# A fused attention and two MoE layers on one core: new step order, sums' guards and weight casts on GpSimd, 29 matmuls halved

## The chip, the cores and the metric

The kernel runs on one NeuronCore of one Trainium2 chip. The metric is the device time of one execution in microseconds. TensorE multiplies (its weight loads have a row of their own, PEld); VectorE is DVE, ScalarE is ACT, GpSimd is POOL and SyncE, which issues the DMAs, is SP in the profile.

## What is computed

Two batches of 12 heads of causal attention (448 tokens, 64 numbers a head), then two layers over the 896 tokens: one with a squared relu, one with the maximum of three products.

```python
scores = q @ k.T / 8;  scores[mask] = -1e9
attn = exp(scores - max(scores));  attn /= sum(attn) + 1e-9
x = (attn @ v)                       # 896 x 768 after joining heads
g = maximum(x @ w_in, 0) ** 2        # 896 x 2048
y = g @ w_out                        # 896 x 768
h = maximum(maximum(y @ w1, y @ w2), y @ w3)
out = h @ w_o                        # 896 x 768
```

q, k and v are float32; the weights arrive as float64 and are put together as float32 on the chip.

## The kernel before

**Attention** works on 12 pairs of heads. A pair's steps are scores (s, TensorE), masked row maxima (m, a custom VectorE instruction that also moves the scores from PSUM into `pr`), exponentials with their sums (e, ScalarE, sums into `st`), the guard 1e-9 on the sums and their reciprocals (r, both on VectorE), the norms (n on GpSimd, n' on VectorE: multiply a row block by its reciprocal), transposes (g, TensorE), their move out of PSUM (h on ScalarE, h' on VectorE) and the product with v (w, TensorE). Row blocks 0 to 6 have 128, 128, 256, 256, 384, 384 and 448 columns; the reciprocals come in three groups a pair (NORM). The output of a pair leaves PSUM by xf or xh (rounded high part) and xl (what the rounding left); sums of such blocks (d) get their own high and low parts (1h to 4h, 1l to 4l).

**Three multiplications** (names f, o and h for w_in, w_out and w1 to w3) use a seven-product scheme for two by two blocks. Every operand is split into a rounded high part and a residual, and a product is three passes, so a step M1 to M7 is nine matmuls of 448 columns. A weight block is loaded into `wr`, then C (`Weight.cast`, ScalarE) spreads the 16 bits on top into the single buffer `up`, and J (`Weight.join`, VectorE) joins it with the rest and issues the next weight load on SP. T1 to T4 (VectorE) form sums of blocks. A quarter of a block gets its high part by H (`Quarter.hi`, ScalarE) and its residual by L (`Quarter.lo`, VectorE) in a ring of five buffers `wq`. XH and XL (also YH, YL, WH, WL, ZH, ZL) do the same to the other operands, S, Y and Z form their sums, and V steps bring results out of PSUM. In the second multiplication M1 of blocks 0 to 3 and M3 of blocks 4 to 7 stay in full precision (`run_full`, line 807). The fourth multiplication, with w_o, is written out behind the order.

**The order** of all steps is the table ORDER. Its entries are issued one by one under a manual schedule, so each engine runs its own steps in the order of the table and waits only for its operands and buffers. In a name such as `H.f3M7` the part behind the point is the block and product, in `e4.5` block 4 of pair 5. Loads of q, k and v are tied to the steps s0 and w0.

Of the kernel before, what the change touches and what calls it, by code (L numbers as in the profile page):

```python
# [28 lines left out]
e6.0 m6.1 m0.1 s4.1 r0.0 m1.1 wload n6'.0 e6.1 m4.1 n4.0 e3.0 r1.0 e0.1 n5.0 e1.1 s2.1 n1.0 n2.0  # L29
g3.0 h3.0 s6.2 m2.1 g0.0 n3'.0 n0'.0 e4.1 m5.1 h0.0 m3.1 r2.1 m6.2 e5.1 g2.0 g1.0 h1'.0 n0.1 s4.2  # L30
s0.2 r0.1 m4.2 m1.2 m0.2 h2.0 w0.0 n4.1 e2.1 w1.0 e6.2 m5.2 n5.1 w2.0 e1.2 n1'.1 n6'.1 w3.0 e4.2
e3.1 s2.2 r1.1 s0.3 m2.2 m3.2 g2.1 e5.2 g0.1 e0.2 e2.2 h2.1 xf.0 e3.2 r0.2 r2.2 n0'.2 g3.1 n1'.2
n5'.2 m0.3 s4.3 m1.3 e0.3 e1.3 m4.3 r1.2 h0.1 m5.3 xh.0 n2.1 s2.3 n3.1 n6.2 n4.2 g1.1 n2'.2 h3.1
m3.3 s6.3 h1.1 n3.2 g3.2 s6.4 m2.3 e3.3 h3'.2 m6.3 g2.2 g1.2 g0.2 s2.4 xl.0 r2.3 e5.3 m6.4 n0'.3
e4.3 s0.4 e6.3 e2.3 m2.4 e6.4 m3.4 r1.3 r0.3 e3.4 n2.3 h1'.2 w0.1 m0.4 w1.1 h2.2 m1.4 w2.1 n3.3
e1.4 n5.3 w3.1 n4.3 s4.4 h0'.2 n1'.3 e2.4 s2.5 m4.4 n6'.3 C.i0 r1.4 g1.3 h1.3 g0.3 g3.3 d3.1 e0.4
n2'.4 m5.4 3h.1 s6.5 m3.5 m2.5 e5.4 m6.5 g2.3 e3.5 s4.5 e4.4 r2.4 s0.5 h0'.3 m1.5 w0.2 w1.2 r0.4
m4.5 n0.4 w2.2 n3.4 e6.5 n1.4 h3.3 e1.5 e2.5 n4.4 n6.4 w3.2 h2'.3 m5.5 m0.5 g1.4 e4.5 s6.6 e5.5
# [18 lines left out]
n1'.11 L.f0M6 h0.10 w0.10 C.i5 w1.10 J.i5 T2.f1 n0.11 2h.7 T3.f0 w2.10 w3.10 3h.9 h1.11 g3.11
g2.11 xh.10 xl.10 h0.11 M2b.f1 M2c.f0 M1c.f1 1l.7 h3.11 T3.f1 T1.f2 d4.7 h2.11 xf.10 w0.11 H.f1M6
2l.7 w1.11 H.f1M3 w2.11 L.f1M6 w3.11 M2c.f1 4h.7 C.i7 L.f1M3 d2.11 2h'.11 V0.f1M1 2l.11 H.f0M7
4l.7 more d1.11 xh.11 L.f0M7 H.f0M5 J.i7 M6.f0 1h'.11 3l.9 M6.f1 V0.f0M6 1l.11 M7.f0 L.f0M5 H.f1M7  # L60
T4.f0 C.i6 H.f1M5 L.f1M7 L.f1M5 H.f0M4 V0.f1M6 J.i6 C.i11 T4.f1 M5.f0 M5.f1 H.f3M1 d4.11 L.f0M4
4h.11 M7.f1 V0.f1M2 V0.f0M7 V1.f1M2 J.i11 xl.11 H.f1M4 V0.f1M7 T1.f3 V2.f1M2 L.f1M4 M4.f0 L.f3M1
# [80 lines left out]
def tile_attention_moe_moe(  # L143
# [23 lines left out]
    nc = tc.nc  # L167
# [227 lines left out]
    class Pair:  # L395
# [126 lines left out]
        def steps(self):  # L522
# [11 lines left out]
            for n, c in enumerate(NORM):  # L534
                e[f"r{n}"] = lambda c=c: self.recip(*c)
# [658 lines left out]
```

## Time and profile before

| what | us |
|---|---|
| three runs | 458.04, 457.92, 455.61; median 457.92 |
| the profiled execution | 456.35 |
| its span, first to last instruction | 454.6 |
| TensorE busy | 447.0 (98%) |
| VectorE busy | 396.3 (87%) |
| ScalarE busy | 324.7 (71%) |
| GpSimd busy | 35.3 (8%) |

Records of matmuls overlap, since a matmul's record holds its way through the array; TensorE's rate is read from the start of one to the start of the next, or from a long stretch divided by its count. The granted clock was full (0.999 in the mean).

### The profile page before, as it was taken

The page shows a single profiled execution, that of the slowest core. Times are in us where ns is not written, and L with a number is a line of the kernel's source. Part 1 is how long each engine was busy: PE and PEld are TensorE (multiplying, and loading weights), DVE is VectorE, ACT ScalarE, POOL GpSimd, SP SyncE. Part 2 cuts the span into 40 slices and gives each one's busy share as a digit, 9 for nine tenths or more (in the row PEclk, how much of TensorE's full clock was granted, in tenths as well). Part 3 has the DMA queues.
Part 4 walks back from the last instruction along what each step waited for, and adds up shares of the span by engine and source line. Part 5 has one row for each costly group of instructions (what it writes and reads, how often), then busy time and mean ns, then how long its engine had stood idle before and what let it go on. Part 6 is the DMA issues. An engine that isn't in the chain of part 4 may idle for free.

```text
span 454.6 us, 6911 instructions
## 1 busy us (share of the span) xinstructions
PE 447.0 (98%) x2338; PEld 384.5 (85%) x2338; DVE 396.3 (87%) x900; ACT 324.7 (71%) x712; POOL 35.3 (8%) x72
## 2 busy tenths in 40 slices
PE   8999999999999999999999999999999999999996
PEld 5676656789999999779999999689999999899996
DVE  5999999999776797999999999999787777788963
ACT  5999999868699899887576777575666455652551
POOL 3424551400000000000000000000000000000000
PEclk9999999999999999999999999999999999999999
DMA  7535274436566666452222534364253023000014
GB/s 219 182 110 185 87 252 122 143 131 183 165 160 189 176 171 193 154 141 69 71 69 69 178 101 145 133 209 138 69 164 116 1 74 136 0 2 0 35 54 156
DMA packets 39395, 56.28 MB, mean 124 GB/s; under 512 B 1728, under 2 KB 31552, under 8 KB 39360
## 3 DMA queue, kind: packets, MB, share of 16 engines
q1 hardware_dynamic: 39072, 55.61, 39.5%
q8 instruction: 18, 0.29, 0.3%
q10 hardware_dynamic: 288, 0.23, 0.1%
q14 instruction: 17, 0.14, 0.1%
HBM read 53.08 MB, written 2.75 MB: 123 GB/s over the span
## 4 chain that ended last, share of the span: by engine, by line
PE 82%; DVE 16%; issue 2%; DVEq 0%
PE ps L575 46%; PE ps L800 19%; PE ps L981 5%; PE ps L807 4%; DVE pr L432 4%; PE ps L421 4%; PE ps L460 2%; PE ps L491 2%; DVE z L202 1%; DVE pr L452 1%; DVE piece L195 1%; DVE wd L202 1%; DVE s L202 1%; DVE wd L255 1%; DVE ph L483 1%
## 5 line engine op out<-in xcount | busy, mean ns | idle before, releaser
L575 PE MATMUL ps<-s,wq 128*128 128x448 f32 x612 | 129.8, 367 | 0.0
L575 PEld LDWEIGHTS ps<-s,wq 128*128 128x128 f32 x612 | 114.7, 188 | 10.6 <-issue 0.4
L575 PE MATMUL ps<-a,wq 128*128 128x448 f32 x459 | 101.2, 369 | 0.3 <-DVE a L195 0.2
L575 PEld LDWEIGHTS ps<-a,wq 128*128 128x128 f32 x459 | 85.3, 188 | 9.2 <-DVE wq L195 0.8
L800 PE MATMUL ps<-x,wq 128*128 128x448 f32 x432 | 88.7, 367 | 0.0
L800 PEld LDWEIGHTS ps<-x,wq 128*128 128x128 f32 x432 | 81.1, 188 | 7.1 <-issue 0.6
L250 ACT CAST up<-wr 128x768 f16<-128x768 bf16 x56 | 60.1, 1074 | 9.3 <-DVE wd L255 2.9
L192 ACT CAST wq<-wd 128x384 fp32r<-128x384 f32 x91 | 45.9, 511 | 25.8 <-PE ps L575 13.1
L255 DVE SCALAR_TENSOR_TENSOR wd<-wr,up 128x768 int32<-128x768 int32 x56 | 54.0, 964 | 9.3 <-ACT up L250 9.3
L195 DVE TENSOR_TENSOR wq<-wd,wq 128x384 fp32r<-128x384 f32 x91 | 49.4, 554 | 7.9 <-ACT wq L192 7.6
L192 ACT CAST wq<-wt 128x384 fp32r<-128x384 f32 x68 | 34.4, 512 | 22.3 <-PE ps L575 20.9
L440 ACT ACTIVATE pr<-pr,st 128x128 f32<-128x128 f32 (+3 forms) x84 | 44.0, 527 | 6.4 <-DVE st L432 6.0
L195 DVE TENSOR_TENSOR wq<-wt,wq 128x384 fp32r<-128x384 f32 x68 | 36.8, 556 | 12.1 <-ACT wq L192 12.0
L432 DVE CUSTOM_DVE_ANT_0 pr<-ps,mask 128x128 f32<-128x128 f32 (+3 forms) x84 | 34.9, 445 | 4.1 <-PE ps L421 3.7
L421 PE MATMUL ps<-k,q 64*128 64x384 f32 (+3 forms) x168 | 36.4, 450 | 1.4 <-DVE st L432 1.2
L452 POOL TENSOR_SCALAR pr<-pr,st 128x384 f32<-128x384 f32 (+3 forms) x59 | 32.8, 570 | 50.2 <-DVE st L448 24.7
L585 ACT COPY s<-ps 128x448 f32<-128x448 f32 x38 | 20.0, 529 | 13.1 <-PE ps L575 11.9
L421 PEld LDWEIGHTS ps<-k,q 64*128 64x128 f32 (+1 forms) x168 | 19.0, 195 | 11.0 <-DVE st L432 5.9
L460 PEld LDWEIGHTS ps<-ident,pr 128*128 128x128 f32 x192 | 21.4, 140 | 7.1 <-issue 3.7
L460 PE MATMUL ps<-ident,pr 128*128 128x128 f32 x192 | 26.3, 277 | 0.0
L195 DVE TENSOR_TENSOR x<-g,x 128x448 fp32r<-128x448 f32 x40 | 24.3, 620 | 0.0
L491 PE MATMUL ps<-ph,v 128*64 128x448 f32 (+3 forms) x192 | 23.4, 386 | 0.5 <-DVE a L195 0.3
(115 smaller groups left out, 568.0 us busy)
## 6 DMA issues: line engine op xcount, KB each, us to landing
wr<-in_moe_w_out SPq DMA_DIRECT2D x22, 768.0 KB, 4.5
wr<-in_moe_w SPq DMA_DIRECT2D x18, 768.0 KB, 4.3
wr<-in_moe_w_in SPq DMA_DIRECT2D x16, 768.0 KB, 4.7
v<-in_v SPq DMA_DIRECT2D x12, 256.0 KB, 3.7
q<-in_q SPq DMA_DIRECT2D x11, 256.0 KB, 2.6
out<-s SPq DMA_DIRECT2D x14, 192.0 KB, 1.9
k<-in_k SPq DMA_DIRECT2D x11, 224.0 KB, 2.8
q<-in_q SPq DMA_DIRECT2D x2, 128.0 KB, 2.8
```

Source lines behind the costliest of these rows:

```text
L192: nc.scalar.copy(hi, src)
L195: nc.vector.tensor_tensor(out=lo, in0=src, in1=hi.bitcast(F32), op=SUB)
L250: nc.scalar.copy(self.up.bitcast(FH)[:, :, 1::2], self.top)
L255: nc.vector.scalar_tensor_tensor(out=self.t.bitcast(I32), in0=self.rest, scalar=13, in1=self.up.bitcast(I32), op0=ALU.logical_shift_right, ...
L421: nc.tensor.matmul(sc[:, :keys[w]], self.n["q"][r, w // 2 * P:(w // 2 + 1) * P], self.n["k"][r, :keys[w]], start=True, stop=True,)
L432: nc.vector.tensor_tensor_reduce(out=self.pr[:, offs[u]:offs[u] + n], in0=self.sc[u][:, :n], in1=mask[:, mask.shape[1] - n:], scale=-SCALE ...
L440: nc.scalar.activation(sl, sl, ACTF.Exp, bias=self.st[:, 0, u:u + 1], scale=-1.0, accum_out=self.st[:, 1, u:u + 1],)
L452: engine.tensor_scalar(sl, sl, self.st[:, 2, u:u + 1], 1.0, op0=ALU.mult, op1=ALU.mult)
L460: nc.tensor.transpose(pt[:, i], self.pr[:, offs[u] + kc * P:offs[u] + (kc + 1) * P], shared["ident"])
L491: nc.tensor.matmul(self.pv[r, kc * P:], self.n["v"][:, kc, r], self.ph[:, h, at], start=kc == 0, stop=kc == NK - 1,)
L575: nc.tensor.matmul(self.acc[n], self.q[n].t[:, ew, i], X[OPERANDS[n]][i][:, ex], start=n in self.starts and i == 0 and e == 0, stop=i == K ...
L800: nc.tensor.matmul(self.acc(n, m), q.t[:, ew, m], x[:, ex], **self.flags(n, j, e == 0, e == 2))
```

## The change

Five things change.

- ORDER is another table (1729 entries in place of 1693). The same steps are done, in another order, and some on another engine.
- The guard on the sums is a step of its own (a on VectorE, a' on GpSimd) ahead of the reciprocal: 10 stay on VectorE, 26 go to GpSimd.
- C and H may run on GpSimd (C' and H'): 15 of 56 C and 72 of 167 H do. Six C' and five H' of them stand ahead of the last step of the attention.
- The high parts of sums that do not run on ScalarE run on GpSimd instead of VectorE: three (five on VectorE before).
- 29 matmuls of 448 columns are issued as two of 224: in each M6 of the first and third multiplications the fifth matmul (17), and in the second multiplication the fifth matmul of each step in three passes of blocks 0 and 4 (12).

```diff
+HALVES = (("M6", 1, 1),)
 ORDER = """
-s0.0 m0.0 m1.0 s2.0 s4.0 m2.0 e1.0 m3.0 m4.0 s6.0 e0.0 m5.0 e2.0 m6.0 e4.0 e5.0 r2.0 s6.1 s0.1
+s0.0 m0.0 s2.0 m1.0 s4.0 e0.0 m2.0 e1.0 s6.0 a2'.0 m3.0 s6.1 e3.0 m4.0 r2.0 m5.0 s0.1 m6.0 e4.0
...
-        def cast(self):
+        def cast(self, copy=nc.scalar.copy):
             _, nk, n = self.shape
             self.up = up[:, :nk * n].rearrange("p (k f) -> p k f", k=nk)
-            nc.scalar.copy(self.up.bitcast(FH)[:, :, 1::2], self.top)
+            copy(self.up.bitcast(FH)[:, :, 1::2], self.top)
...
+            todo[f"H'.{name}"] = lambda: self.hi(nc.gpsimd.tensor_copy)
+
+        def hi(self, copy=act_hi):
             self.t = wp.tile([P, 2, KH, P], FR, tag="q", name="wq", bufs=RING)
-            act_hi(self.t[:, 0], self.src())
+            copy(self.t[:, 0], self.src())
...
+        def guard(self, engine, c0, c1):
+            st, cs = self.st, slice(c0, c1)
+            engine.tensor_scalar_add(st[:, 2, cs], st[:, 1, cs], 1.0e-9)
+
         def recip(self, c0, c1):
             st, cs = self.st, slice(c0, c1)
-            nc.vector.tensor_scalar_add(st[:, 2, cs], st[:, 1, cs], 1.0e-9)
             nc.vector.reciprocal(st[:, 2, cs], st[:, 2, cs])
...
+                e[f"a{n}"] = lambda c=c: self.guard(nc.vector, *c)
+                e[f"a{n}'"] = lambda c=c: self.guard(nc.gpsimd, *c)
...
+                ("'", nc.vector.tensor_copy, nc.gpsimd.tensor_copy),
...
+                    e[f"{n}h{way}"] = lambda n=n, copy=other: self.sum_hi("s" + n, copy)
...
+    def matmul_in_parts(acc, w, x, at, **flags):
+
+        for c in (slice(0, at), slice(at, S)):
+            if c.start < S:
+                nc.tensor.matmul(acc[:, c], w, x[:, c], skip_group_check=True, **flags)
...
+                        S // 2 if (n, i, e) in HALVES else S,
...
+                        S // 2 if (j % 4, m, e) == (0, 1, 1) else S,
```

VectorE in the attention, where the row maxima of blocks 2 and 3 of the third pair are taken (`pr_102` holds its rows, `st` its sums). Before:

```order
L432 ISA pr_102,st<-ps_71,mask_89 128x256
L432 ISA st 128x1
L432 ISA pr_102,st<-ps_68,mask_89 128x256
L432 ISA st 128x1
L447 TENSOR_SCALAR st<-st 128x3
L448 RECIPROCAL st<-st 128x3
L447 TENSOR_SCALAR st<-st 128x2
L448 RECIPROCAL st<-st 128x2
L452 TENSOR_SCALAR pr_102<-pr_102,st 128x128 x2
L452 TENSOR_SCALAR pr_102<-pr_102,st 128x384
```

After:

```order
L453 TENSOR_SCALAR st<-st 128x3
L457 RECIPROCAL st<-st 128x3
L438 ISA pr_102,st<-ps_71,mask_89 128x256
L438 ISA st 128x1
L438 ISA pr_102,st<-ps_68,mask_89 128x256
L438 ISA st 128x1
L457 RECIPROCAL st<-st 128x2
L492 COPY ph<-ps_74 128x2x2x128
```

One of the two guards here, and the three norms (L452 before, L461 now), have left VectorE; a reciprocal (L457) stands alone.

GpSimd from the end of the attention into the first multiplication (`up` is the buffer of C, `wq` the ring of quarters). Before, its list ends there:

```order
L452 TENSOR_SCALAR pr_103<-pr_103,st 128x256
L452 TENSOR_SCALAR pr_103<-pr_103,st 128x384 x2
L452 TENSOR_SCALAR pr_103<-pr_103,st 128x128
L1189 UNCONDITIONAL_BRANCH
```

After:

```order
L255 CAST up<-wr 128x768
L276 CAST wq<-wt 128x384
L276 CAST wq<-wd 128x384 x2
L276 CAST wq<-wt 128x384 x2
L255 CAST up<-wr 128x768
L276 CAST wq<-wd 128x384
L276 CAST wq<-wt 128x384
```

Casts that stood on ScalarE now follow one another on GpSimd, down to the end of the third multiplication.

TensorE at M6 of the first block of the first multiplication. Before:

```order
L575 MATMUL ps_68<-s_748,wq 128x448 x3
L575 MATMUL ps_68<-s_1087,wq 128x448 x3
L575 MATMUL ps_68<-s_1155,wq 128x448 x3
```

After:

```order
L572 MATMUL ps_68<-s_692,wq 128x448 x3
L572 MATMUL ps_68<-s_1084,wq 128x448
L572 MATMUL ps_68<-s_1084,wq 128x224 x2
L572 MATMUL ps_68<-s_1084,wq 128x448
L572 MATMUL ps_68<-s_1154,wq 128x448 x3
```

The fifth of the nine has become two of half the columns; the others stand as they were.

## Rows read from the trace of the kernel before

**Rows 1.** The page: span, and section 1, each engine's busy us and count.

```profile
span 454.6 us, 6911 instructions
PE 447.0 (98%) x2338; PEld 384.5 (85%) x2338; DVE 396.3 (87%) x900; ACT 324.7 (71%) x712; POOL 35.3 (8%) x72
```

**Rows 2.** Busy time by stage; the first line names the columns.

```profile
core 0: us, PE busy (x) PEld busy (x) DVE busy (x) ACT busy (x) POOL busy (x), PEclk, DMA share, GB/s
0.00:17.60 17.60, 16.30 (x90) 10.83 (x91) 12.35 (x59) 12.72 (x40) 6.20 (x20) 1.00 0.71 216
17.60:93.60 76.00, 73.79 (x508) 50.18 (x507) 74.06 (x273) 70.41 (x209) 29.07 (x52) 1.00 0.49 154
93.60:186.00 92.40, 92.40 (x455) 84.68 (x454) 76.53 (x137) 78.72 (x151) 0.00 (x0) 1.00 0.59 171
186.00:297.30 111.30, 111.30 (x510) 95.51 (x509) 108.72 (x204) 79.92 (x153) 0.00 (x0) 1.00 0.36 110
297.30:410.70 113.40, 113.40 (x561) 104.39 (x559) 92.67 (x171) 66.36 (x125) 0.00 (x0) 1.00 0.27 88
```

**Rows 3.** The chain in order of time: start us, us, what.

```profile
93.61 92.66 PE ps L575 x453
...
200.75 72.95 PE ps L800 x360
...
288.30 9.02 PE ps L807 x24
...
432.00 19.01 PE ps L981 x108
```

**Rows 4.** Groups by form on VectorE: xcount | busy us, mean ns | idle before.

```profile
L447 DVE TENSOR_SCALAR st<-st 128x2 f32<-128x2 f32 x24 | 5.2, 216 | 0.4 <-ACT pr L440 0.4
L447 DVE TENSOR_SCALAR st<-st 128x3 f32<-128x3 f32 x12 | 2.1, 172 | 0.0
L452 DVE TENSOR_SCALAR pr<-pr,st 128x128 f32<-128x128 f32 x10 | 3.6, 367 | 0.0
L452 DVE TENSOR_SCALAR pr<-pr,st 128x384 f32<-128x384 f32 x3 | 1.5, 496 | 0.0
L452 DVE TENSOR_SCALAR pr<-pr,st 128x448 f32<-128x448 f32 x6 | 3.0, 505 | 0.0
L517 DVE CAST s<-s 128x448 fp32r<-128x448 f32 x5 | 2.1, 428 | 0.0
L502 DVE CAST a<-ps 128x448 fp32r<-128x448 f32 x3 | 1.8, 612 | 0.0
```

**Rows 5.** Groups by form on ScalarE, 0 to 93.6 us.

```profile
L250 ACT CAST up<-wr 128x768 f16<-128x768 bf16 x7 | 7.5, 1074 | 0.0
L192 ACT CAST wq<-wd 128x384 fp32r<-128x384 f32 x5 | 2.6, 515 | 0.0
```

**Rows 6.** Groups by form on GpSimd, 44.9 to 47.4 us.

```profile
L452 POOL TENSOR_SCALAR pr<-pr,st 128x384 f32<-128x384 f32 x2 | 1.2, 586 | 5.3 <-DVE st L448 5.3
L452 POOL TENSOR_SCALAR pr<-pr,st 128x128 f32<-128x128 f32 x2 | 0.7, 372 | 0.0
```

**Rows 7.** VectorE and GpSimd in order of time; guards of the sums by duration.

```profile
39.04 0.64 POOL L452 TENSOR_SCALAR pr<-pr,st 128x448 f32<-128x448 f32 x1
39.15 1.33 DVE L255 SCALAR_TENSOR_TENSOR wd<-wr,up 128x768 int32<-128x768 int32 x1
...
82.70 2.65 POOL L452 TENSOR_SCALAR pr<-pr,st 128x384 f32<-128x384 f32 x2
82.71 0.54 DVE L202 TENSOR_TENSOR wt<-wd 128x384 f32<-128x384 f32 x1
83.28 0.82 DVE L202 TENSOR_TENSOR wt<-wd,wt 128x384 f32<-128x384 f32 x1
84.03 0.95 DVE L255 SCALAR_TENSOR_TENSOR wd<-wr,up 128x768 int32<-128x768 int32 x1
...
L447 DVE TENSOR_SCALAR st<-st x36: 148/164/515, 8.5 to 85.5; 128x2 f32<-128x2 f32 x24, 128x3 f32<-128x3 f32 x12
```

More of the change, by code (lines that the diff above doesn't have):

```diff
@@ L33 @@
[L33 to L38, printed above, removed]
@@ L57 @@
[L57 to L62, printed above, removed]
@@ new lines @@
+V0.f0M1 3h.9 C'.i5 w3.10 xf.10 xh.10 1l.7 g1.11 xl.10 J.i5 g2.11 h1.11 2l.7 h2.11 g3.11 M2b.f1
+M2c.f0 h3.11 C.i7 w0.11 T4.f0 H'.f1M6 w1.11 L.f1M6 w2.11 w3.11 M1c.f1 d2.11 M2c.f1 d1.11 2h.11
+2l.11 more L.f0M7 J.i7 V0.f1M1 M6.f0 1h.11 H.f1M5 L.f1M5 M6.f1 T4.f1 T3.f1 H.f0M5 1l.11 M5.f1
+L.f0M5 H.f0M4 C.i6 3l.9 xh.11 J.i6 T1.f2 H.f2M1 L.f2M1 M5.f0 H.f1M7 L.f0M4 d4.11 L.f1M7 V0.f0M6
+M7.f0 V0.f1M6 xl.11 C.i11 H'.f3M1 4h.11 H'.f1M4 M7.f1 V0.f0M7 H.f1M3 4l.11 L.f3M1 L.f1M4 J.i11
+M4.f0 C'.i10 V0.f1M7 L.f1M3 V1.f1M7 M4.f1 M3.f1 V0.f1M4 J.i10 M1.f3 T3.f3 V0.f1M2 T1.f3 T2.f2
@@ new lines @@
+XL.o1M3 XH.o7M5 XH.o5M7 XL.o1M4 XL.o7M5 M6.o5 H'.o3M7 M6.o6 T3.o2 H.o1M7 J.a0 L.o7M5 M6.o7 L.o3M7
+T4.o4 XH.o2M7 T3.o4 XL.o7M7 M5.o7 V0.oM6 V1.oM6 XL.o2M7 L.o1M7 H.o4M7 H.o0M7 L.o0M7 XH.o6M7
+XH.o2M4 V2.oM6 XL.o5M7 H.o2M7 L.o2M7 C.b1 T4.o6 J.b1 XH.o3M4 S4.o6 M7.o0 XL.o6M7 H.o7M7 C.a1
+XH.o0M3 T4.o0 S4.o5 M7.o1 L.o4M7 T4.o5 T4.o2 XH.o7M4 H.o1M4 XH.o0M4 XL.o2M4 M7.o2 M7.o3 H.o5M7
+H.o6M7 L.o5M7 L.o7M7 M7.o4 H'.o2M4 XH.o4M4 M7.o5 L.o6M7 J.a1 C.b0 L.o2M4 T4.o7 M7.o6 XL.o3M3
+L.o1M4 XL.o4M4 M7.o7 V0.oM7 H'.o0M4 L.o0M4 XL.o0M4 V1.oM7 XL.o3M4 V4.oM7 V2.oM7 J.b0 V3.oM7
@@ new lines @@
+H.h1M4 L.h1M4 M2.h1 V0.h0M2 J.a4 V0.h1M2 M4.h1 M1.h2 YH.s42 V0.h1M4 H.h3M1 V0.h2M1 L.h2M6 C.c3
+YH.s41 L.h3M1 T2.h3 V1.h0M7 M1.h3 H'.h3M7 Y4.0 H.h3M6 L.h3M7 H.h1M3 YL.s42 M6.h2 V0.h3M1 J.c3
+YH.s40 H.h2M7 V0.h2M6 L.h3M6 M6.h3 T1.h4 C.z1 L.h2M2 T1.h5 T4.h3 H'.h2M5 YL.s40 YL.s41 M2.h2
+L.h2M7 V0.h3M6 T2.h5 H'.h0M3 L.h1M3 V1.h1M7 M7.h3 M7.h2 J.z1 L.h0M3 T4.h2 C.b4 M3.h0 H.h2M4 J.b4
+T2.h4 H'.h3M2 H.h5M1 V0.h2M7 V1.h1M2 C.a5 T4.h5 L.h2M4 L.h2M5 L.h3M2 V0.h3M7 M3.h1 V0.h0M3 V0.h1M3
+M4.h2 J.a5 H'.h3M4 H'.h4M1 M5.h2 C'.b5 V0.h2M2 H.h4M6 M2.h3 H.h3M5 L.h3M4 J.b5 L.h4M6 M4.h3
@@ L139 @@
+V1.h5M3 H.h7M4 L.h7M7 H'.h8M7 WL.2 ZL.31 ZH.30 M7.h7 V0.h6M3 M5.h8 L.h8M7 L.h7M4 WL.1 ZL.30
+V0.h7M7 V2.h5M7 V0.h8M6 H.h8M4 M4.h7 L.h8M4 V1.h7M7 ZH.l ZL.l ZL.0 H'.h8M3 M7.h8 M3.h7 WH.5 WL.0
+V2.h7M7 V0.h8M7 V1.h8M7 L.h8M3 M3.h8 V0.h7M3 Z2.l V0.h7M4 WL.5 M4.h8 Z1.l M.2 V1.h7M3 M.0 Z4.l
+V0.h8M3 WL.4 V2.h8M7 WL.3 V1.h8M3 V0.h8M4 M.1 V.1 V.0 V.2
 """
@@ L231, in __init__ @@
             todo[f"C.{name}"], todo[f"J.{name}"] = self.cast, self.join
+            todo[f"C'.{name}"] = lambda: self.cast(nc.gpsimd.tensor_copy)
             blocks[name] = self
@@ L539, in steps @@
                 e[f"g{g}"] = lambda g=g: self.probs(g)
-            for way, copy in (("", nc.scalar.copy), ("'", nc.vector.tensor_copy)):
+            for way, copy, other in (
+                ("", nc.scalar.copy, nc.scalar.copy),
+                ("'", nc.vector.tensor_copy, nc.gpsimd.tensor_copy),
+            ):
                 e["xf" + way] = lambda copy=copy: self.x_full(copy)
@@ L574, in run @@
                 for e, (ew, ex) in enumerate(PASSES):
-                    nc.tensor.matmul(
+                    matmul_in_parts(
                         self.acc[n], self.q[n].t[:, ew, i], X[OPERANDS[n]][i][:, ex],
-                        start=n in self.starts and i == 0 and e == 0,
-                        stop=i == KH - 1 and e == 2, skip_group_check=True,
+                        S // 2 if (n, i, e) in HALVES else S,
+                        start=n in self.starts and i == 0 and e == 0, stop=i == KH - 1 and e == 2,
                     )
@@ L799, in run @@
                 for e, (ew, ex) in enumerate(PASSES):
-                    nc.tensor.matmul(
-                        self.acc(n, m), q.t[:, ew, m], x[:, ex], **self.flags(n, j, e == 0, e == 2)
+                    matmul_in_parts(
+                        self.acc(n, m), q.t[:, ew, m], x[:, ex],
+                        S // 2 if (j % 4, m, e) == (0, 1, 1) else S,
+                        **self.flags(n, j, e == 0, e == 2),
                     )
@@ L807, in run_full @@
                 nc.tensor.matmul(
-                    self.acc(n, m), self.wt(n, j)[:, m], self.xt(n, j), **self.flags(n, j, True, True)
+                    self.acc(n, m), self.wt(n, j)[:, m], self.xt(n, j), skip_group_check=True,
+                    **self.flags(n, j, True, True),
                 )
@@ L1057, in tile_attention_moe_moe @@
     order = ORDER.split()
-    line += [blocks[n[2:]] for n in order if n.startswith("C.")]
+    line += [blocks[n.split(".")[1]] for n in order if n[0] == "C"]
     for i in range(3):
```

192 lines of the change are left out of this document (91 added, 101 removed).

## The prediction

> **What bounds the kernel now.** I read these views, in this order. The page's first section says that TensorE is busy for 447.0 of 454.6 us, VectorE for 87% and GpSimd for 8% [rows 1]. These are averages over stages with different limits, so the second view is the table of busy times by stage [rows 2]. From 93.6 us on TensorE is busy in every microsecond up to 410.7; before that it is not: in 17.60 to 93.60, the attention, VectorE is busy for 74.06 of 76.00 us and ScalarE for 70.41, and TensorE's 73.79 there is not work at its rate, because records of small matmuls overlap.
>
> The third view is the chain in order of time [rows 3]. Up to 93.6 us it alternates between short pieces of VectorE and TensorE; then it is one stretch of TensorE alone, 453 matmuls in 92.66 us (204.5 ns each), later 360 in 72.95 us (202.6 ns each), and at the end 108 of 384 columns in 19.01 us (176 ns each). So the span is the attention's length plus about 361 us in which TensorE is never late. A cut made behind 93.6 us brings nothing, because no other engine is waited for there; work added there costs nothing either, until VectorE or ScalarE falls behind. In the attention it is VectorE that sets the pace, with ScalarE close behind.
>
> **Guards, norms and copies that leave VectorE.** I counted the steps up to the last attention step of TensorE (w3.11) in both orders; the multiplication work in that part is the same but for three matmuls (the third part of M1 of f1, which before does ahead of w3.11 and after does behind it).
> - Guards: 26 of 36 go to GpSimd. They take 216 and 172 ns, 24 and 12 of them [rows 4], mean 201: 26 x 0.201 = 5.2 us less.
> - Norms on VectorE: 128 wide 10 to 3, 256 wide 6 to 6, 384 wide 3 to 8, 448 wide 6 to 2. With 367, 496 and 505 ns [rows 4]: -2.6 + 2.5 - 2.0 = -2.1 us.
> - Casts of the sums: the five at 428 ns leave VectorE [rows 4], -2.1 us (three go to GpSimd, the rest to ScalarE).
> - Copies of the attention's output out of PSUM: three of 612 ns before [rows 4], one after, -1.2 us. Moves of transposed probabilities nearly cancel.
>
> Together 10.8 us. VectorE's busy time up to 93.6 us falls from 12.35 + 74.06 = 86.4 to 75.6 us.
>
> **Casts that leave ScalarE in the attention.** Of its casts of weights, five of 1074 ns and five of 515 ns go to GpSimd [rows 5], -7.9 us; it takes over two casts of sums and two copies of the output, at the nearest row's 515 ns [rows 5] +2.1 us. Its busy time up to 93.6 us falls from 12.72 + 70.41 = 83.1 to 77.3 us. So ScalarE, not VectorE, is then the fuller engine.
>
> What does this make of the 93.6 us? If the old idle time of VectorE (7.2 us) stays, 75.6 + 7.2 = 82.8, a gain of 10.8. If the old idle time of ScalarE (10.5 us) stays and ScalarE sets the pace, 77.3 + 10.5 = 87.8, a gain of 5.8. I take 8.5 us, a little above the middle, since part of ScalarE's idle time was waiting for VectorE. TensorE has room: its weight loads are busy for 10.83 + 50.18 = 61.0 of these 93.6 us [rows 2]. What is late next: ScalarE's exponentials and the hop that the guards now make. A guard on GpSimd waits for ScalarE's sum, the reciprocal on VectorE waits for the guard, and behind the reciprocal stand the next row maxima of VectorE, which TensorE's scores wait for. GpSimd has room: 128 columns take 372 ns and 384 take 586 [rows 6], so 0.84 ns a column, which puts a guard at about 0.27 us, a cast of 384 columns at 0.59 and one of 768 at 0.91 (estimates from these rows). With 65 norms, 26 guards, 6 + 5 casts of weights and 3 of sums it is busy for some 54 us of 85.
>
> **Casts on GpSimd behind the attention.** There GpSimd did nothing [rows 2]; now it gets 76 casts: 31 while the first multiplication fills TensorE (93.6 to 186), 13 in the second, 32 after it. ScalarE loses 67 x 0.51 + 9 x 1.07 us, which is worth nothing, since TensorE waited for nobody. The question is what they do to VectorE. Nearly all its work here reads two operands in SBUF, and the rows show what happens when GpSimd reads too. A subtraction that takes 0.54 us took 0.82 beside a GpSimd norm, a join that takes 0.95 took 1.33, and two GpSimd norms of 384 columns took 2.65 us instead of 1.17 [rows 6, 7]; a guard on two numbers, 164 ns in the median, took up to 515 [rows 7]. So whoever comes second waits. Bounds for one cast: 0, where GpSimd does the waiting or falls into an idle moment of VectorE, and 0.59, where VectorE waits for the whole cast, as the residual behind it must. I take 0.27 (0.82 - 0.55) for a cast of 384 and 0.38 (1.33 - 0.95) for one of 768 columns. VectorE's idle time in the three stages is 15.9, 2.6 and 20.7 us [rows 2]; the casts add 26 x 0.27 + 5 x 0.38 = 8.9, 13 x 0.27 = 3.5, and 28 x 0.27 + 4 x 0.38 = 9.1. Only the second stage overflows, by 0.9 us. The order puts some casts right ahead of their residual, with no VectorE instruction between, and the ring holds five pairs of weights, so I add 2 us for places where TensorE catches up: 3 us in all (bounds 0 and 11).
>
> The Trainium skill ("SBUF — State Buffer", section "Who interferes with whom") says that GpSimd and VectorE share one pair of ports, that a VectorE instruction with two SBUF inputs takes it against a GpSimd instruction that reads SBUF, and that the loser is blocked for the whole instruction. The 1.33 us join agrees; by that rule each cast in a dense stretch may cost its whole length, which is rival 1.
>
> **Halved matmuls.** 29 matmuls of 448 columns become two of 224 (17 in the first and third multiplications, 12 in the second), all where TensorE has no idle time. The spacing is 202.6 ns for 448 and 176 for 384 columns [rows 3]: 0.415 ns a column and 16.6 ns for each matmul. Two halves cost 16.6 ns more, 29 x 0.0166 = 0.5 us. The trace has no matmul of this type under 256 columns. Upper bound: the untouched full-precision matmuls of 448 columns, 24 in 9.02 us, 376 ns each [rows 3]; at that rate the pair costs 174 ns more, 5.0 us in all. A gain has no reason: the same columns pass. I take 0.6, nearest the row of the same type.
>
> **The rest of the order.** The three matmuls that slip behind w3.11 add 0.6 us to TensorE's stretch. Every join still issues one weight load, 56 as before, on SP's queue, and loads of q, k and v are tied to the same steps; the weights come in the new order of their casts. Cost nothing, while a load lands well ahead of its cast; if GpSimd's cast is late, its join, the next load and the next cast are late with it, since there is one buffer for the cast.
>
> **Sum**, against the profiled execution's own 456.35 us (span 454.6 and 1.75 around it): 456.35 - 8.5 + 3.0 + 0.6 + 0.6 = 452.05, so **452.0 us**. That execution lies 1.6 us under the median of the three runs, 457.92, and their spread is 2.4 us; I do not correct for it.
>
> **The rivals.**
> 1. The ports decide: slower. Every cast behind the attention costs VectorE its whole length, 0.59 or 0.91 us. Then the stages get 26 x 0.59 + 5 x 0.91 = 19.9 us against 15.9 idle, 7.7 against 2.6, and 20.2 against 20.7: with little to even them out TensorE waits for 9 to 11 us, and the same contention halves the gain in the attention. 456.35 - 4.2 + 11 + 1.2 = 464.3 us. It decides from about 0.45 us for each cast. For it: VectorE is busy for 108.72 of 111.30 us in the second stage, with two-operand work. Against it: in the rows GpSimd did most of the waiting.
> 2. The hop takes the gain: same. Guards come late because norms stand ahead of them in GpSimd's queue, and ScalarE sets the pace: 2.5 us gained, 456.35 - 2.5 + 3.0 + 1.2 = 458.05 us.
> 3. Matmuls of 224 columns run at the full-precision rate: 452.0 + 4.4 = 456.4 us, same.
> 4. Everything fits: 10.8 us gained, no stall behind it: 456.35 - 10.8 + 1.1 = 446.7 us.
>
> **How the numbers follow.** Forecast (449 to 455.5 us) 0.50, rival 4 and better 0.16, rivals 2 and 3 together 0.15, rival 1 0.19. A measurement of this kernel can tell about 0.5% from no change, so faster means under 455.6 and slower over 460.2 us. The forecast and rival 4 are faster: 0.66; rivals 2 and 3 the same: 0.15; rival 1 slower: 0.19. For 8 in 10 the range takes in rivals 2 to 4 and the near third of rival 1: 445 to 461 us.
>
> **What would show it.** Right: the long stretch of TensorE alone begins near 85 us instead of 93.6; VectorE's busy time up to there near 76 us and ScalarE's near 78; behind it no idle time of TensorE over 1 us but near the second multiplication; pairs of 224 columns spaced by about 109 ns. Rival 1: VectorE busy for 98% and more in all stages behind the attention, with residuals over 0.7 us, and TensorE waiting for them. Rival 2: VectorE's reciprocals waiting for GpSimd's guards. Rival 3: the halves 187 ns apart. I would be wrong altogether if the attention did not get shorter although VectorE has 10 us less to do.

## The result, and the profile after

The changed kernel takes 451.27 us (median of four runs, 450.96 to 451.52) beside 457.14 of the kernel before on the same chip: a ratio of 0.9875, with a 95% interval of 0.9842 to 0.9907. It is faster, by 5.9 us; 452.0 was forecast. The profiled execution took 451.45 us, 4.9 less than that of the kernel before; its span is 449.7. But the parts of the sum did not come out as forecast: two large ones were wrong, in opposite directions.

The page of the changed kernel (span; busy us of each engine, its share and its count; the chain by engine):

```profile
span 449.7 us, 7054 instructions
...
PE 444.2 (99%) x2367; PEld 385.1 (86%) x2367; DVE 400.3 (89%) x860; ACT 282.2 (63%) x630; POOL 126.8 (28%) x194
...
PE 92%; DVE 3%; ACT 2%; POOL 1%; issue 1%; POOLq 0%; ACTq 0%
```

GpSimd went from 35.3 to 126.8 us, ScalarE from 324.7 to 282.2 [rows 1]. The busy times by stage (columns as in [rows 2], cut at the places where the same work ends now):

```profile
0.00:17.60 17.60, 16.43 (x91) 10.92 (x92) 11.60 (x54) 12.79 (x42) 7.69 (x25) 1.00 0.67 216
17.60:89.40 71.80, 71.16 (x504) 48.49 (x502) 67.56 (x238) 64.48 (x199) 50.51 (x94) 1.00 0.49 153
89.40:182.20 92.80, 92.80 (x465) 86.14 (x466) 82.17 (x137) 62.96 (x121) 24.48 (x32) 1.00 0.58 165
182.20:293.00 110.80, 110.80 (x523) 96.24 (x522) 107.71 (x199) 73.16 (x138) 17.44 (x13) 1.00 0.39 123
293.00:406.80 113.80, 113.80 (x567) 104.65 (x566) 101.03 (x178) 51.37 (x95) 26.69 (x31) 1.00 0.26 87
```

Up to 89.40 VectorE is idle for 10.2 us now (17.60 - 11.60 + 71.80 - 67.56), up to 93.60 it was idle for 7.2 before: its work fell by 7.2 us, and 3.0 of them became idle time. The chain in order of time (start us, us, what) shows who sets the pace now:

```profile
45.18 1.88 PE ps L500 x16
47.06 1.46 PE ps L469 x12
48.52 1.99 PE ps L427 x12
...
58.60 2.61 ACT pr L446 x10
...
64.50 1.50 ACT ph L492 x4
...
78.89 0.87 DVE wd L260
...
81.64 1.55 POOL pr L461 x2
...
89.38 92.77 PE ps L572 x464
```

From 17.3 to 55.8 us the chain is TensorE alone (L427 scores, L469 transposes, L500 products with v), where before it alternated with VectorE; from 55.9 to 85.2 it changes between VectorE, ScalarE and GpSimd. The long stretch begins at 89.38 us, not at 93.61 [rows 3]: 4.2 us earlier. What follows it takes 449.7 - 89.4 = 360.3 us, where before it took 454.6 - 93.6 = 361.0.

GpSimd's new instructions and those that wait for it, in groups by form:

```profile
L276 POOL CAST wq<-wd 128x384 fp32r<-128x384 f32 x41 | 34.5, 841 | 137.9 <-PE ps L572 108.8 <-DVE x L199 8.0 <-DVE wq L199 7.6
L276 POOL CAST wq<-wt 128x384 fp32r<-128x384 f32 x30 | 23.5, 786 | 93.7 <-PE ps L572 79.2 <-issue 7.1 <-DVE wt L206 4.2
L453 POOL TENSOR_SCALAR st<-st 128x2 f32<-128x2 f32 x18 | 5.7, 319 | 8.7 <-ACT pr L446 7.8
L457 DVE RECIPROCAL st<-st 128x2 f32<-128x2 f32 x24 | 3.7, 158 | 0.5 <-POOL st L453 0.3
L457 DVE RECIPROCAL st<-st 128x3 f32<-128x3 f32 x12 | 2.1, 172 | 0.6 <-POOL st L453 0.4
L199 DVE TENSOR_TENSOR wq<-wd,wq 128x384 fp32r<-128x384 f32 x91 | 53.1, 592 | 8.8 <-POOL wq L276 5.6 <-ACT wq L196 3.0
L199 DVE TENSOR_TENSOR wq<-wt,wq 128x384 fp32r<-128x384 f32 x68 | 40.9, 610 | 9.4 <-POOL wq L276 5.9
```

The same casts by duration (ns: least/median/longest; first and last start):

```profile
L276 POOL CAST wq<-wd x41: 498/662/2799, 47.1 to 397.7; 128x384 fp32r<-128x384 f32 x41
L276 POOL CAST wq<-wt x30: 501/603/2722, 85.1 to 394.1; 128x384 fp32r<-128x384 f32 x30
```

A cast of 384 columns takes 0.50 us at least and 0.60 to 0.66 in the median, near the 0.59 of the estimate; the means of 0.79 and 0.84 come from a few of 1.7 to 2.8 us. A guard on two numbers takes 0.32 us. The reciprocals wait 0.7 us in all for guards. The two groups of residuals take 592 and 610 ns and wait 5.6 and 5.9 us in all for GpSimd's casts, and yet TensorE waits for none of it: behind 89.4 us no wait of its matmuls is on record.

### The profile page after: what moved, and what is told of

It reads as the page before. It is cut to its first block, busy times and chain, and to the rows that moved or that the text cites. A ratio compares the mean times of both kernels' runs of the same rounds, so it can differ in the third digit from the quotient of the medians.

```text
span 449.7 us, 7054 instructions
## 1 busy us (share of the span) xinstructions
PE 444.2 (99%) x2367; PEld 385.1 (86%) x2367; DVE 400.3 (89%) x860; ACT 282.2 (63%) x630; POOL 126.8 (28%) x194
## 4 chain that ended last, share of the span: by engine, by line
PE 92%; DVE 3%; ACT 2%; POOL 1%; issue 1%; POOLq 0%; ACTq 0%
PE ps L572 67%; PE ps L1003 7%; PE ps L427 6%; PE ps L828 4%; PE ps L469 4%; PE ps L500 3%; PE ps L1106 1%; ACT pr L446 1%; DVE pr L438 1%; DVE wt L206 1%; ACT ph L492 1%; DVE wd L260 1%; PE ps L1068 1%; POOL pr L461 1%; DVE s L199 0%
## 5 line engine op out<-in xcount | busy, mean ns | idle before, releaser
L572 PE MATMUL ps<-s,wq 128*128 128x448 f32 (+1 forms) x629 | 130.1, 361 | 0.0
L572 PE MATMUL ps<-x,wq 128*128 128x448 f32 (+1 forms) x444 | 88.6, 361 | 0.0
L276 POOL CAST wq<-wd 128x384 fp32r<-128x384 f32 x41 | 34.5, 841 | 137.9 <-PE ps L572 108.8
L255 ACT CAST up<-wr 128x768 f16<-128x768 bf16 x41 | 44.2, 1078 | 18.4 <-DVE wd L260 13.3
L276 POOL CAST wq<-wt 128x384 fp32r<-128x384 f32 x30 | 23.5, 786 | 93.7 <-PE ps L572 79.2
L461 POOL TENSOR_SCALAR pr<-pr,st 128x128 f32<-128x128 f32 (+3 forms) x65 | 37.5, 589 | 13.0 <-DVE st L457 10.9
L438 DVE CUSTOM_DVE_ANT_0 pr<-ps,mask 128x384 f32<-128x384 f32 (+3 forms) x84 | 35.3, 444 | 5.9 <-PE ps L427 4.6
L196 ACT CAST wq<-wd 128x384 fp32r<-128x384 f32 x50 | 25.5, 513 | 23.2 <-PE ps L572 22.5
L427 PE MATMUL ps<-k,q 64*128 64x128 f32 (+3 forms) x168 | 35.2, 452 | 0.0
L196 ACT CAST wq<-wt 128x384 fp32r<-128x384 f32 x38 | 19.4, 512 | 19.9 <-PE ps L572 17.0
L469 PEld LDWEIGHTS ps<-ident,pr 128*128 128x128 f32 x192 | 21.4, 140 | 7.6 <-issue 4.2
L469 PE MATMUL ps<-ident,pr 128*128 128x128 f32 x192 | 26.0, 277 | 0.6 <-POOL pr L461 0.6
L427 PEld LDWEIGHTS ps<-k,q 64*128 64x128 f32 (+1 forms) x168 | 17.8, 197 | 8.7 <-DVE st L438 3.6
```

Of the source, the lines that this page charges most:

```text
L196: nc.scalar.copy(hi, src)
L255: copy(self.up.bitcast(FH)[:, :, 1::2], self.top)
L276: copy(self.t[:, 0], self.src())
L427: nc.tensor.matmul(sc[:, :keys[w]], self.n["q"][r, w // 2 * P:(w // 2 + 1) * P], self.n["k"][r, :keys[w]], start=True, stop=True,)
L438: nc.vector.tensor_tensor_reduce(out=self.pr[:, offs[u]:offs[u] + n], in0=self.sc[u][:, :n], in1=mask[:, mask.shape[1] - n:], scale=-SCALE ...
L461: engine.tensor_scalar(sl, sl, self.st[:, 2, u:u + 1], 1.0, op0=ALU.mult, op1=ALU.mult)
```

## The experiments

"Stretch" is the start of the long TensorE stretch behind the attention. Where small waits cut it up (marked *), it is the start of the first matmul behind the last product with v, a time that lies 0.1 us ahead of the stretch in the other kernels. Each ratio is to the kernel before, run beside it on the same chip.

| kernel | median us | ratio (95%) | stretch |
|---|---|---|---|
| changed | 451.27 | 0.9875 (0.9842 to 0.9907) | 89.38 |
| e1 guards on VectorE | 453.98 | 0.9941 (0.9925 to 0.9957) | 91.67 |
| e2 late casts on ScalarE | 463.32 | 1.0154 (1.0130 to 1.0177) | 88.77 |
| e3 early casts on ScalarE | 453.41 | 0.9928 (0.9911 to 0.9945) | 90.64 |
| e4 whole matmuls | 452.52 | 0.9909 (0.9886 to 0.9932) | 88.42 |
| e5 new order, old engines | 467.56 | 1.0221 (1.0176 to 1.0267) | 93.33* |
| e6 old order, new engines | 461.7 | 1.0106 (1.0072 to 1.0140) | not read |
| e7 changed, one pass | 451.87 | 0.9875 (0.9834 to 0.9917) | 89.14* |
| e8 before, one pass | 456.57 | 0.9991 (0.9965 to 1.0018) | 89.93* |
| e9 changed, block 6 twice | 458.82 | 1.0051 (1.0032 to 1.0070) | 96.39 |
| e10 before, block 6 twice | 462.22 | 1.0116 (1.0085 to 1.0147) | 98.92 |
| e11 before, halves | 457.68 | 1.0011 (0.9995 to 1.0028) | 93.91* |
| e12 before, late casts on GpSimd | 460.08 | 1.0066 (1.0043 to 1.0090) | 92.83* |

**The guards (e1).** In all 26 places:

```diff
-a2'.0 m3.0 s6.1 e3.0 m4.0 r2.0
+a2.0 m3.0 s6.1 e3.0 m4.0 r2.0
```

> The changed kernel with its 26 GpSimd guards put back on VectorE, at the same places of the order. Theory (VectorE's relief shortened the attention until TensorE's own small matmuls became the limit there): 5.2 us of VectorE work come back, part of it hidden behind TensorE, so the long stretch of TensorE alone starts 2 to 4.5 us later than 89.4 us and the time is 453.3 to 455.8 us. Rival (the new order did it, whichever engine does the guards): the stretch starts within 1 us of 89.4 and the time stays under 452.3 us.

2.7 us slower, and the stretch begins 2.3 us later, as expected. The busy times of this kernel (columns as above):

```profile
0.00:17.60 17.60, 16.32 (x95) 11.09 (x96) 12.51 (x59) 13.38 (x44) 7.50 (x23) 1.00 0.72 217
17.60:91.67 74.07, 72.77 (x501) 48.55 (x499) 69.51 (x259) 64.63 (x197) 43.09 (x70) 1.00 0.48 148
```

VectorE is busy for 12.51 + 69.51 = 82.0 us up to the stretch here, for 11.60 + 67.56 = 79.2 in the changed kernel. The records of the 26 guards add up to 5.3 us, but they overlap the records beside them, so 2.9 us of VectorE's busy time went with them. The time follows these 2.9 us almost in full; it is the 5.2 that counted too much.

**The late casts (e2).** The 76 casts behind the attention return to ScalarE, in the same places of the order:

```diff
-M4.f0 C'.i10 V0.f1M7
+M4.f0 C.i10 V0.f1M7
...
-J.i9 V1.f0M2 H.f2M2 H'.f3M7 L.f2M2
+J.i9 V1.f0M2 H.f2M2 H.f3M7 L.f2M2
```

> The changed kernel with the 76 casts of weights behind the attention put back on ScalarE. Theory (TensorE waits for nobody there, before or after): 451.3 us within 0.7 us, ScalarE about 48 us busier, VectorE some 10 us less busy. Rival, the shared ports (the casts on GpSimd hold VectorE back and this reaches TensorE): 1.5 us or more faster. Rival, ScalarE (its queue would have made TensorE wait): 1.5 us or more slower, with TensorE waiting for high parts of weights.

My theory fell, and the rival on ScalarE's queue came true: 12 us slower than the changed kernel, with the stretch's start 0.6 us earlier. The loss lies behind the attention: between the same places of the chain the first multiplication takes 7.6 us more, the second 1.0 and the third 3.6. The busy times of this kernel there:

```profile
89.40:182.20 92.80, 88.53 (x433) 78.94 (x432) 69.54 (x126) 72.71 (x140) 0.00 (x0) 1.00 0.52 152
182.20:293.00 110.80, 109.60 (x524) 96.21 (x523) 104.55 (x196) 80.83 (x156) 0.00 (x0) 1.00 0.39 121
293.00:406.80 113.80, 111.94 (x540) 99.33 (x538) 92.30 (x172) 67.12 (x127) 0.00 (x0) 1.00 0.30 98
```

TensorE, never idle there in the changed kernel, waits 4.3, 1.2 and 1.9 us as records go, which overlap and hide a part. Its waits (who waits, for whom: us in all, count, longest):

```profile
ACT wq L195 <- PE ps L571: 40.6, 49, 2.0
DVE wq L198 <- ACT wq L195: 33.4, 24, 5.1
...
PEld ps L571 <- DVE wq L198: 5.4, 8, 1.1
```

The cast waits for TensorE to free its place in the ring, the residual on VectorE for the cast, TensorE's weights for the residual. ScalarE is busy for 78% and less of these stages, but these are means. From 120 to 130, 150 to 160 and 170 to 190 us it is busy for 9.1 to 9.4 of each 10 us, and there the chain runs through its own work:

```profile
150.44 0.40 ACT wq L195
150.84 0.44 ACT g L631
151.28 0.94 ACT g L635 x2
152.21 0.43 ACT g L631
...
153.40 1.09 ACT up L254
```

So two things can cost here: ScalarE is full in places, and elsewhere everything in its list stands behind a cast that waits for the ring. The runs don't tell their shares apart. A list of their own (GpSimd's) removes both: the casts wait there without holding up the moves out of PSUM and the casts of the other operands.

**The early casts (e3).** The six C' and five H' ahead of the attention's last step return to ScalarE:

```diff
-a1'.3 C'.i0 a2.3
+a1'.3 C.i0 a2.3
...
-h2'.5 H'.f0M2 m5.7
+h2'.5 H.f0M2 m5.7
```

> The changed kernel with the 6 + 5 casts of weights ahead of the end of the attention put back on ScalarE. Theory (ScalarE is next in line behind VectorE): 8 us of work come back to ScalarE, which was busy for 77 of 89.4 us, so the long stretch starts 1.5 to 4 us later, 452.8 to 455.3 us. Rival (VectorE or TensorE alone set the pace): within 0.7 us of 451.3.

2.1 us slower, as expected; 1.3 of them lie at the stretch's start, just under the 1.5 to 4 expected there.

**The halves (e4, e11).** Whole matmuls in the changed kernel, and the same halves in the kernel before:

```diff
-HALVES = (("M6", 1, 1),)
+HALVES = ()
...
-                        S // 2 if (j % 4, m, e) == (0, 1, 1) else S,
+                        S,
```

> The changed kernel with the 29 halved matmuls whole again. Theory (a pair of halves takes 215 ns where a whole one takes 203): 0.4 us less, 450.9 us. Rival (the halves keep TensorE from losing time elsewhere): 1 us or more slower, with matmuls spaced by over 212 ns where the changed kernel has none.

> The kernel before with only the 29 halved matmuls. By the spacing in the changed kernel's trace a pair of halves takes 12.5 ns more than a whole, so 0.4 us: I expect no difference that can be told, 456.5 to 458 us. The question is the spread: the runs of the kernel before lie 4 us apart, those of the changed kernel 0.6, those of the changed kernel with whole matmuls 4. If the halves steady the time, the runs of this kernel lie within 1.5 us; if not, they lie 3 to 4 us apart, like those of before.

Neither moves the time by what can be told: 1.3 us (0.28%) between the medians of e4 and of the changed kernel, with overlapping intervals; 0.1% for e11. In the changed kernel's trace the two halves start 102 and 113 ns before what follows, together 215, where a whole takes 203: 12 ns for each of 29, 0.36 us. The runs of e4 lay 4.0 us apart (450.42 to 454.45), those of the changed kernel 0.6; but the twelve of e11 lay 2.2 us apart. So the halves don't steady the time by themselves, and what sets the spread stays open.

**Order and engines apart (e5, e6).** e5 is e1, e2 and e3 together with the three sums' casts on ScalarE; e6 is the old table with the new letters:

```diff
-r2.0
+a2'.0 r2.0
...
-H.f3M7
+H'.f3M7
```

> The changed kernel in its new order and with its halves, but every cast, copy and guard back on the engine that it had before (71 quarters' high parts, 15 casts of the loaded weights, 26 guards and three sums' casts leave GpSimd). My theory now: the new order was made for the casts on GpSimd, so order and engines bring nothing apart. The late casts alone cost 12.0 us when they went back to ScalarE, the guards 2.7, the early casts 2.1; together, without credit for overlap, 451.3 + 16.8 = 468; I expect 463 to 471 us, with the long stretch of TensorE beginning between 92 and 96 us and then several stalls. Rival: the order itself is the better one and the engines matter little; then 452 to 457 us.

> The old order, without halves, with the engines of the change: the same 72 + 15 casts on GpSimd, 26 guards on GpSimd right ahead of their reciprocals, three sums' casts on GpSimd. The norms stay where the old order had them. My theory: the old order puts VectorE's reciprocal right behind a guard that now makes a hop over GpSimd, and its residuals right behind casts that take 0.8 us instead of 0.5, so the engines' relief is lost to waits: the long stretch begins at 92 to 97 us instead of 93.6, and behind it TensorE waits for 1 to 6 us: 457 to 466 us. Rival: relief of VectorE and ScalarE alone is the gain, and it does not need the order: the stretch begins before 91 us, 450 to 454 us.

Both came out in the expected range. Alone, the new order costs 2.2% and the new engines cost 1.1%; together they gain 1.25%. The profiled execution of e6 took 1128.69 us, where the other five took 461.04 to 462.10, so its trace isn't read. Added up as if independent, the two would have given some 473 us; the pair is 21 us better than that. So neither the order nor the engines have a price of their own. The split isn't a full one: which norms, moves and copies out of PSUM VectorE does goes with the order in both kernels, and no run tests these apart.

**The late casts alone (e12).** The old order and old engines, with only the 76 late casts on GpSimd:

```diff
-H.f3M7
+H'.f3M7
...
-C.i10
+C'.i10
```

> The old order and the old engines, without halves, but the same 76 casts behind the attention on GpSimd (67 quarters' high parts, 9 of the loaded weights). This is the price of the late casts by themselves, which I had forecast at 3 us (0 to 11). The old order with all engine choices of the change took 461.7, 5 us more than before. Theory: these casts take 0.8 us on GpSimd, and the old order leaves no distance between a cast and its residual, so VectorE and then TensorE wait: the stretch begins at 93 to 94 us as before, stalls of 2 to 6 us behind it, 458 to 462 us. Rival: the old order's loss lies in the attention (guards right ahead of reciprocals), and the late casts cost nothing in any order: 456 to 457.5 us.

0.66% slower (0.43 to 0.90%), 3.0 us of 456.6 by the ratio, as the theory had it; the stretch begins 0.7 us earlier than before. 3.0 us is what I had forecast for these casts, but in the order for which I had taken the prices. One place where they cost (time line of e12: start us, us, engine, operation, tiles):

```profile
260.92 4.29 POOL L276 CAST wq<-wd 128x384 fp32r<-128x384 f32 x1 [13.07 <-PE ps L572]
...
261.21 0.62 DVE L199 TENSOR_TENSOR a<-y,a 128x448 fp32r<-128x448 f32 x1
261.75 0.55 DVE L199 TENSOR_TENSOR wq<-wd,wq 128x384 fp32r<-128x384 f32 x1
...
262.22 0.62 DVE L199 TENSOR_TENSOR x<-g,x 128x448 fp32r<-128x448 f32 x1
262.75 1.02 DVE L206 TENSOR_TENSOR wt<-wd 128x384 f32<-128x384 f32 x2
...
263.69 1.15 DVE L199 TENSOR_TENSOR x<-g,x 128x448 fp32r<-128x448 f32 x2
...
266.15 0.56 DVE L199 TENSOR_TENSOR wq<-wd,wq 128x384 fp32r<-128x384 f32 x1 [1.31 <-POOL wq L276]
...
273.58 0.68 PE L572 MATMUL ps<-x,wq 128*128 128x448 f32 x2 [1.21 <-DVE x L199]
```

This GpSimd cast lasts 4.29 us: VectorE runs two-operand instructions back to back until 264.84 us, and the cast ends at 265.21. Two short casts behind it end at 266.1; then VectorE's residual has waited 1.31 us for them. VectorE isn't idle again before TensorE, in its turn, waits 1.21 us for it. VectorE is not slowed in this run; it is stopped afterwards. The changed kernel has the same thing (its time line):

```profile
233.40 3.74 POOL L276 CAST wq<-s 128x384 fp32r<-128x384 f32 x1 [3.65 <-PE ps L572]
...
237.17 0.56 DVE L199 TENSOR_TENSOR wq<-s,wq 128x384 fp32r<-128x384 f32 x1 [0.40 <-POOL wq L276]
```

Here other VectorE work stood between, the residual waited 0.40 us, and TensorE for nothing.

These are not chance pairs. Of the 72 such casts of the changed kernel, 19 have no VectorE instruction with two operands in SBUF beside them, and none of these takes more than 0.51 us. The seven longest take 1.7 to 3.7 us, and each is as long as the time for which VectorE is busy with such instructions beside it, plus 0.37 us. VectorE pays as well, a little at a time: from the stretch's start to the end its busy time is 321.1 us in the changed kernel and 308.7 in e2, 321.8 in e12 and 309.9 in the kernel before. That is some 12 us for 76 casts, 0.16 us for each.

**TensorE's share of the attention (e7 to e10).** Less work for TensorE:

```diff
-                    self.pv[r, kc * P:], self.n["v"][:, kc, r], self.ph[:, h, at],
+                    self.pv[r, kc * P:], self.n["v"][:, kc, r].bitcast(BF)[:, 1::2],
+                    self.ph[:, h, at].bitcast(BF)[:, 1::2],
```

(and the same for q and k in the scores), in the changed kernel and in the one before:

> The changed kernel, but the scores and the products with v read only the upper 16 bits of q, k, v and of the transposed probabilities (as bfloat16), so that these two kinds of products are computed more coarsely and TensorE needs one pass for them. Nothing else is touched. My theory: in the changed kernel TensorE's own small matmuls set the pace of the attention from 17 to 56 us; VectorE's relief was worth only 4.2 us because TensorE came next. Then the long stretch begins 2 to 8 us earlier than 89.4 us and the time falls to 443 to 449 us. Rival: ScalarE and the hops between engines set the pace; TensorE only looks busy because it is always waited with; then the stretch stays within 1 us of 89.4 and the time at 450.5 to 452.

> The kernel before with the same edit: scores and products with v from the upper 16 bits alone, so computed more coarsely, in one pass. In the kernel before VectorE set the pace (74 of 76 us busy). My theory: relief of TensorE is worth little there: the stretch begins within 1.5 us of 93.6, 455.5 to 457.5 us. Rival: TensorE limited the kernel before as well, and my reading of its 61 us of weight loads as room was wrong for both; then the stretch begins 3 us or more earlier and the time is below 454.

e7 came out as the rival had it, not as my theory did: TensorE's busy time from 17.60 to 89.40 fell from 71.16 to 55.40 us, and the attention ended where it had. But the test is not clean. Two stretches of e7 (columns as above; the granted clock stands third from the right):

```profile
22.00:24.00 2.00, 1.29 (x11) 0.93 (x8) 1.94 (x8) 2.00 (x9) 0.94 (x2) 1.00 0.41 111
24.00:26.00 2.00, 1.47 (x10) 0.72 (x10) 1.97 (x13) 2.00 (x8) 0.91 (x2) 1.00 0.41 115
26.00:28.00 2.00, 1.40 (x12) 0.47 (x10) 1.52 (x8) 1.23 (x5) 1.82 (x5) 0.80 0.28 99
28.00:30.00 2.00, 1.39 (x7) 1.42 (x8) 2.00 (x8) 2.00 (x9) 1.36 (x3) 0.50 1.01 297
...
17.60:89.40 71.80, 55.40 (x355) 40.42 (x354) 65.41 (x235) 63.11 (x198) 50.39 (x93) 0.81 0.47 149
```

From 22 to 28 us TensorE was busy for 1.29 to 1.47 of each 2.0 us; then its granted clock fell from 1.00 to 0.50, the lower of its two levels (1.2 GHz). The mean over the attention is 0.81, and the untouched transposes took 341 ns instead of 277 in the mean. In e8 the clock's mean in the attention is 0.86, so it isn't clean either. There the attention ended 3.6 us earlier (89.93), as the rival had it, but the time stayed, as my theory had it: TensorE then waited for sums and weights. The chain of e8:

```profile
98.03 0.94 DVE wq L195 x2
98.96 0.88 DVE wd L255
99.89 5.22 DMA wr<-in_moe_w_in
105.19 1.08 ACT up L250
...
107.13 78.30 PE ps L577 x378
```

From 89.90 to 107.10 us VectorE is busy for 16.70 of 17.20 us. So in the old order its preparation of weights and sums is not done when the attention ends early, and relief of TensorE alone brings nothing. The opposite edit leaves TensorE at its full clock (1.00 in both):

```diff
-                nc.tensor.matmul(
+                for _ in range(2 if u == 2 * NQ else 1):
+                    nc.tensor.matmul(
```

> The changed kernel, with the scores of block 6 (448 columns, 0.75 us of TensorE) issued twice in each of the 12 pairs; the second overwrites the first, so the values are the same. 9.1 us more for TensorE, seven of the twelve (5.3 us) between 17 and 56 us, and TensorE stays at the full clock, which the one-pass run did not. My theory: between 17 and 56 us TensorE sets the pace in the changed kernel, so these 5.3 us are paid in full and the others in part: the long stretch begins at 94.5 to 98 us instead of 89.4, 456.5 to 460 us. Rival: VectorE and ScalarE (35 of 38 us busy there) set the pace and TensorE only follows: the stretch begins before 92, below 454 us.

> The kernel before with the same edit, 9.1 us more for TensorE in the attention. My theory: VectorE paced it there, so most of the added work falls into TensorE's waits: the stretch begins at 94 to 97 us instead of 93.6 (less of the added work is paid than in the changed kernel), 457 to 460 us. Rival: TensorE was the limit before as well: the stretch begins at 99 us or later, above 462 us.

Two pieces of e9's chain, its first product with v and its stretch:

```profile
15.96 1.88 PE ps L501 x16
...
96.39 92.78 PE ps L573 x464
```

Of 9.1 us added, the changed kernel pays 7.0 at the stretch's start (96.39 for 89.38), the kernel before 5.3 (98.92 for 93.61). e9 came out as my theory had it; e10 lies between the two theories (its 462.22 us just on the rival's side, its stretch just short of it): TensorE was nearer to the limit before than I had thought. The clean comparison starts at the first product with v, since three of the twelve matmuls lie ahead of it. From there to the stretch e9 takes 80.43 us (96.39 - 15.96) and the changed kernel 74.79 (89.38 less 14.59, where its chain has that product): 5.6 more for nine matmuls of 0.75, 6.8 us. In that part of e9 the chain is TensorE but for 0.5 us. So TensorE's own work takes 80.4 - 0.5 - 6.8 = 73.1 us, or 73.6 with that half microsecond, and with the changed kernel's start the stretch can't begin before 87.7 to 88.2 us. The changed kernel is 1 to 2 us above this floor, and e4 begins at 88.42 us, close to it. With e10 the same part went from 78.9 to 82.4 us (98.92 - 16.56): 3.4 of the 6.8 us were paid, and the rest fell into waits.

## Why the prediction was right, and where it was not

Against the profiled execution: 456.35 - 4.2 (the stretch's start) - 0.7 (behind it) = 451.45 us, its time. I had -8.5, +3.0, +0.6 and +0.6. The 452.0 is right by luck in good part: a gain twice too large and a cost that did not come nearly cancel.

- **The attention, 8.5 forecast, 4.2 measured.** Two steps failed. The first is the size of VectorE's relief: 10.8 us forecast, 7.2 measured (86.4 to 79.2 us, not to 75.6). I had added up durations of records, and short records overlap: the guards' 5.2 us were 2.9 of busy time (e1). Also, two of the five casts of sums at 428 ns start behind the attention, so -2.1 should have been about -1.4. The second is "TensorE has room", from weight loads busy for 61.0 of 93.6 us. Weight loads are only a part of what a small matmul costs. The better row was at hand: records of matmuls busy for 73.79 of 76.00 us [rows 2], which I had put aside because records overlap. A start of 85 us lies below the floor of 87.7 to 88.2 that e9 gives. Either error alone would have kept the gain under 8.5 us; the runs don't share out the miss between them. The causes of the gain were the right ones: guards (2.7 us by e1) and early casts (2.1 by e3) are most of it, and ScalarE's busy time came to 77.3 us, as worked out.
- **Late casts, 3.0 forecast, no wait measured.** The size was right for the order in which I had priced it (e12: 3.0 us, 2.0 to 4.1), but 2 of the 3 us were a margin. VectorE does lose a little beside the casts, 0.16 us each where I had 0.27 and 0.38. The rows I had it from show the other case too: the subtraction of 0.54 us also ran beside a norm. And GpSimd's own waiting, which I had put at 0, comes back: now and then it is shut out for microseconds, and VectorE then waits at the residual. In the new order this wait doesn't reach TensorE.
- **"Which is worth nothing", of ScalarE's relief behind the attention.** In the old order TensorE waited for nobody; in the new one the same casts on ScalarE cost 12.0 us (e2). I had taken the change's parts as separable: e5 and e6 show that they are not.
- **Halves, 0.6 forecast, 0.36 measured**, and the three moved matmuls 0.6. What follows the stretch's start became 0.7 us shorter in spite of these 1.0, so some 1.7 us went from there. I had read TensorE as never late behind 93.6 us, and that was wrong for the end: from 410.69 to 432.00 us the chain of before is VectorE's, 21.3 us, and its counterpart, 406.76 to 427.14, is 20.4 us of TensorE. These 0.9 us are over half of the 1.7; the rest is a difference, not seen gap by gap. The upper bound for the halves rested on a misreading: the chain's 24 are records, two for each full-precision matmul, so 752 ns each.
- **The rivals.** 1 (ports) had VectorE lose 0.59 us or more beside each cast, and it lost 0.16; the one that is shut out is GpSimd, for up to 4.3 us in e12, with the wait handed on. The Trainium skill ("SBUF — State Buffer", "Who interferes with whom") has the loser blocked for a whole instruction; here it was for a run of seven. 2 (the hop) is out: 0.7 us of waits for guards, and 4.2 us gained where it had 2.5. 3 is out at 215 ns a pair. 4 had the right second half, no stalls, and a first half that TensorE forbids.

## What to carry to other kernels

Don't price a relief by adding up durations of short instructions: their records overlap, so read what they add to the engine's busy time. Before a relief of the pacing engine is priced, find the floor of the next one by doubling a known piece of its work: what is paid shows how near it is, and doubling kept the clock up here (e9, e10) where removing did not (e7, e8). In a hand-written order an operation's price on another engine holds for that order only; ask where it stands in that engine's list and how far behind it its reader stands. A cast that waits for a buffer is better not put into a list ahead of work that could go on.

## What the runs showed of the hardware

- TensorE's clock fell to its lower level in the attention when its work there was cut (e7: 0.81 in the mean, 55.40 of 71.80 us busy), and stood at 1.00 there in the changed kernel and in e9, with more work.
- A GpSimd cast of 384 columns, 0.50 us at its shortest, lasted 4.29 and 3.74 us beside close runs of two-operand VectorE instructions, while these kept their 0.55 to 0.62 us each. Without such an instruction beside it none of 19 took more than 0.51 us; the seven longest took as long as VectorE was busy with them, plus 0.37 us.
- Two matmuls of 224 columns took 12 ns more than one of 448 (215 and 203).
- 26 small VectorE instructions with records of 0.2 us each moved VectorE's busy time by 2.9 us (e1), since their records overlap their neighbours'.
